# Two mixture-of-experts layers behind linear attention: layer 2's first expert on split weights with the slots stationary, and slot products and copies moved at the end of attention

## The chip, the cores and the metric

The kernel runs on one core of a Trainium2 chip, as one program. The metric is the device time of one execution in microseconds (us). The engines are TensorE (PE in the rows; its weight loads are PEld), VectorE (DVE), ScalarE (ACT), GpSimd (POOL) and SyncE (SP), each with a queue of its own that it works off in order. They wait for each other by semaphores. Loads and stores go through 16 DMA engines, fed by queues on SP, ACT and POOL.

## The reference

Input are q, k, v of 2 batches x 8 heads x 768 positions x 64, and for each of two layers a gate (512 x 8) and the weights w1 (8 x 512 x 1024) and w2 (8 x 1024 x 512) of eight experts, all f32. Linear attention with a decay comes first:

```python
for t in range(S):
    state = gamma[None, :, None, None] * state + np.einsum('bhd,bhe->bhde', k[:, :, t], v[:, :, t])
    y[:, :, t] = scale * np.einsum('bhd,bhde->bhe', q[:, :, t], state)
```

Its output is 1536 tokens of 512 features. Each of the two layers then sends a token to its best expert alone:

```python
expert_idx = np.argmax(x @ w_gate, axis=1)
h = np.maximum(xe @ w1[e], 0.0)        # xe: the tokens of expert e
out[mask] = gate_w[mask, None] * (h @ w2[e])
```

`gate_w` is the softmax probability of the chosen expert. In layer 2 an expert takes its first 384 tokens only and the rest give zero.

## The kernel before, in words

**Tiling.** Tokens go in 12 tiles of 128. Attention ends with the logits of each tile's rows; `step(n, 0..2)` routes tile n: key and one-hot, rank among the tokens of its expert, and the place in the expert's list of slots. The rows of a layer's input lie in memory (`x1d` for layer 1, `x2d` for layer 2), and an indirect DMA of POOL, the gather (L347), fetches the rows of an expert's slots. Each expert has up to 256 slots in the kernel's layout, in tiles of 128 (the second one may be shorter).

**Weights.** An expert has eight slices of 128 x 1024 (512 KB): four of w1 and four of w2. A slice is loaded into `st` by SP, cast by ACT to a short f32 format, `whi` (L159), and DVE subtracts to get the rest, `wlo` (L170). A product then takes three matmuls: x·hi, x·lo and the rest of x times hi. The expert that comes first in a layer is chosen early (`choose`), before all tokens are routed. Its four w1 slices are loaded whole (`load_whole`), without cast and subtraction, and multiplied in full f32 (`products`, L434, weights stationary, 128 or 112 slots moving). Slices are numbered through: 0 to 63 are layer 1's, 64 to 127 layer 2's; slices 64 to 67 are the w1 of layer 2's first expert. SP's load of slice 72 and all behind it waits for the gather of the first expert's second tile.

**The two boundaries.** While the last tokens of a layer's input are routed, PE would have nothing to do. There the products of the first expert's first 128 slots are put between the routing's small matmuls (`ahead_of`, `ahead[1](n)`; each call issues one of eight groups of four f32 matmuls, which the trace shows as eight rows). When the last placement is through (`ig`, L245), `of_first` (L407, L411) picks the row numbers of the second tile, and POOL gathers these rows. `finish_route` (DVE, some 18 small instructions to `over`, L311) sorts the experts and writes the slot lists; the relus (`hidden`: ACT L457, DVE L458) and further products are mixed into it. When the second tile's rows are there, PE turns them (`first_x`, L377), ACT copies them (L378), and the products of the second tile follow. In layer 1, `second()` puts 24 warming matmuls of no use (L374) ahead of that. In layer 2, the output of the first tile (`o_part`, L859 to L861) stands between.

**The last expert.** Layer 2's last expert already does what the change does elsewhere: `hidden_rows` (L820 to L822) keeps the slots stationary and moves 256 columns of the split weights, twelve matmuls per slice; `back_hidden` turns the result back by four transposes (L828), a cast by ACT (L830) and a subtraction by DVE (L831), which give h and its rest. Here the relu comes before (L999).

**What sets the order.** The program is written out in order, so each engine's order is the order of the calls. `between(j, i)` is called after each eighth of an expert and hands out casts and subtractions of the slices to come.

Of the kernel before, what the change touches and what calls it, by code (L numbers as in the profile page):

```python
# [10 lines left out]
F32 = mybir.dt.float32  # L11
F32R = mybir.dt.float32r
# [6 lines left out]
P = 128  # L19
# [60 lines left out]
def fused(ctx, tc, qT, kT, vkr, wg, w11, w12, w21, w22, cst, out, capacity):  # L80
# [44 lines left out]
    def whole(q):  # L125

        return q // 8 % E == 0 and q % 8 < 4
# [343 lines left out]
    with tc.tile_pool(name="ap", bufs=3) as ap:  # L471
# [352 lines left out]
    def back_hidden(hr, h, b):  # L824
# [4 lines left out]
        sl = slice(4 * b, 4 * b + 4)  # L829
        A.copy(h[:, sl, 0, :P], tp)  # L830
        V.tensor_sub(h[:, sl, 1, :P], tp, h[:, sl, 0, :P])  # L831
# [47 lines left out]
    def layer(li, xd, rin):  # L879
# [4 lines left out]
        h = xp.tile([P, KF, 2, C0], F32R, tag="h", name="h", bufs=1)  # L884
# [3 lines left out]
        left = []  # L888
# [7 lines left out]
        def second():  # L896
            x[0] = first_x(rows[0][1], 24)
            go(1)

# [9 lines left out]
        if li == 0:  # L909
            ix = finish_route(rin, li, [None, None, lambda: evac(0), None, None, done])  # L910
            second()
            split()
            evac(1)
            done()
        else:
            ix = finish_route(rin, li, [lambda: evac(0), None, None, done, None, None, lambda: (go(1), evac(1)), None,
                                        done])
            split()
        next_rows(1)
        if li == 1:  # L920
            gate[0][0][0]()
            ps0 = mmtile("o")
            o_part(E * 8, P, h, [ps0], range(0, 6))
            gate[0][0] = gate[0][0][1]()
            x[0] = first_x(rows[0][1])
            o_part(E * 8, P, h, [ps0], range(6, KF))
            put_out(0, 0, P, ps0, gate[0][0][0], ix)

        def between(j, i):
# [29 lines left out]
            if li == 0 and j + 1 == E and i == 4:  # L959
                rt[1]["x"] = first_x(rt[1]["rows"])  # L960
# [6 lines left out]
        def rows_first(j):  # L967

            return li == 1 and j + 1 == E and caps[j] == P

        for j in range(E):
# [6 lines left out]
            for i in range(4):  # L978
                if j == 0:
# [10 lines left out]
                elif rows_first(j):  # L990
                    if i % 2 == 0:
                        ps = mmtile("hr")
                    hidden_rows(q0, x[j], i, ps)
                    run_pend()
                    if i == 2:
                        back_hidden(hr, h, 0)
                    if i % 2:
                        hr = xp.tile([P, 2, C0], F32, tag="hs", name="hr", bufs=2).rearrange("p a c -> p (a c)")
                        A.activation(hr, ps, AF.Relu)  # L999
# [12 lines left out]
            if li == 0:  # L1012
# [7 lines left out]
                for d2 in range(2):  # L1020
# [91 lines left out]
            else:  # L1112
                tiles = halves(cap)[j == 0:]
                ps = [mmtile("o")[:c] for _, c in tiles]
                for i in range(4):
                    o_part(q0, cap, h, ps, (2 * i, 2 * i + 1), int(j == 0))
                    between(j, 4 + i)
# [233 lines left out]
class Halves:  # L1351
# [7 lines left out]
    def half(self, i, bank, xt):  # L1359
# [6 lines left out]

        part = self.rp.tile([P, E], F32, tag=f"lg{i}", name=f"lg{i}")[:self.cnt]
# [7 lines left out]
        o = self.row[:, i * 2 * P:(i + 1) * 2 * P].rearrange("p (j c) -> p j c", j=2)  # L1375
        if gate is None:
            nc.scalar.copy(o, v[:, :, 0:P])
        else:
            nc.scalar.activation(o, v[:, :, 0:P], AF.Copy, scale=gate)
# [46 lines left out]
```

## Time and profile before

| | |
|---|---|
| median of 3 runs | 427.5 us (424.79 to 427.71) |
| profiled execution | 428.34 us, span of its instructions 426.6 us |
| granted TensorE clock, mean | 0.991 |
| PE / weight loads | busy 407.3 us (95%) / 382.0 us |
| DVE | busy 319.1 us (75%) |
| ACT | busy 239.3 us (56%) |
| POOL | busy 96.5 us (23%) |

Times in the rows count from the first instruction of the profiled execution. The boundary from attention to layer 1 lies at about 61 to 74 us, that from layer 1 to layer 2 at 231 to 278 us.

### The profile page before, as it was taken

How to read it: one execution, taken by the hardware profiler on the slowest of the kernel's cores; microseconds unless marked ns; L12 is line 12 of the kernel's file. 1: busy time of each engine (PE TensorE's matmuls, PEld its weight loads, DVE VectorE, ACT ScalarE, POOL GpSimd, SP SyncE). 2: the span in 40 equal slices, each digit the busy share in tenths (PEclk: the TensorE clock that was granted, in tenths of full speed). 3: DMA queues.
4: the chain of work that ended last, by engine and by line, in shares of the span. 5: the costliest groups of instructions: out<-in, count | busy, mean ns of one | idle time of the engine just before them, and what ended most of it. 6: DMA issues, size and time to landing. Idle time of an engine off the chain costs nothing.

```text
span 426.6 us, 9472 instructions
## 1 busy us (share of the span) xinstructions
PE 407.3 (95%) x3403; PEld 382.0 (90%) x3403; DVE 319.1 (75%) x870; ACT 239.3 (56%) x485; POOL 96.5 (23%) x89
## 2 busy tenths in 40 slices
PE   8999989999999999999999999999999999999980
PEld 7887869999999999999999998998889999999970
DVE  3678786788889898989798954677585878787710
ACT  2111221667766666677665622666666787878620
POOL 2334214104041323222100313021304122301120
PEclk9999999999999999999999999999999999999996
DMA  8999974976757576776658615578757777776310
GB/s 316 388 385 390 339 312 136 354 260 223 222 189 246 209 241 226 233 234 231 191 197 265 236 35 190 210 272 284 272 181 253 247 264 241 245 277 233 128 48 16
DMA packets 32503, 100.45 MB, mean 235 GB/s; under 512 B 4669, under 2 KB 5181, under 8 KB 32448
## 3 DMA queue, kind: packets, MB, share of 16 engines
q1 hardware_dynamic: 25488, 82.74, 56.1%
q0 software_dynamic: 4656, 13.00, 8.8%
q10 hardware_dynamic: 2304, 4.02, 2.5%
q8 instruction: 29, 0.48, 0.4%
q14 instruction: 26, 0.21, 0.2%
HBM read 87.01 MB, written 12.99 MB: 234 GB/s over the span
## 4 chain that ended last, share of the span: by engine, by line
PE 80%; DMA 9%; DVE 3%; issue 3%; SPq 1%; ACT 1%; POOL 1%; POOLq 0%; ACTq 0%; DVEq 0%
PE y L844 17%; PE h L800 17%; PE h L801 8%; PE y L845 8%; PE h L434 7%; PE cb L1332 4%; DMA vk<-vkr 3%; PE o L859 3%; PE o L861 3%; PE o L860 3%; PE tp L362 2%; DMA whole<-w 2%; DMA qb<-qT 2%; DMA rows<-x1d,eig 2%; DVE wlo L170 1%
## 5 line engine op out<-in xcount | busy, mean ns | idle before, releaser
L170 DVE TENSOR_TENSOR wlo<-st,whi 128x1024 fp32r<-128x1024 f32 x120 | 145.1, 1217 | 4.1 <-ACT x L378 2.6
L159 ACT CAST whi<-st 128x1024 fp32r<-128x1024 f32 x120 | 125.0, 1045 | 24.9 <-DMA st<-w 24.5
L844 PE MATMUL y<-h,whi 128*128 128x416 f32 (+9 forms) x384 | 116.9, 369 | 0.0
L800 PE MATMUL h<-x,whi 128*128 128x416 f32 (+9 forms) x384 | 114.5, 365 | 0.0
L845 PE MATMUL y<-h,wlo 128*128 128x208 f32 (+9 forms) x384 | 96.9, 252 | 0.0
L801 PE MATMUL h<-x,wlo 128*128 128x208 f32 (+9 forms) x384 | 96.7, 252 | 0.0
L844 PEld LDWEIGHTS y<-h,whi 128*128 128x128 f32 x384 | 72.1, 188 | 2.5 <-DVE rro L232 0.4
L800 PEld LDWEIGHTS h<-x,whi 128*128 128x128 f32 x384 | 72.1, 188 | 2.1 <-issue 0.6
L801 PEld LDWEIGHTS h<-x,wlo 128*128 128x128 f32 x384 | 73.4, 191 | 0.1
L845 PEld LDWEIGHTS y<-h,wlo 128*128 128x128 f32 x384 | 73.4, 191 | 0.0
L321 POOL DMA_INDIRECT x2d<-row,is x16 | 17.4, 1088 | 117.1 <-ACT row L1345 87.7
L812 DVE SCALAR_TENSOR_TENSOR h<-hs,h 128x416 fp32r<-128x416 f32 (+9 forms) x48 | 27.0, 562 | 19.1 <-ACT h L811 15.7
L321 POOL DMA_INDIRECT out<-ob,is x14 | 14.9, 1067 | 111.9 <-ACT ob L865 109.4
L811 ACT ACTIVATE h<-hs 128x416 fp32r<-128x416 f32 (+9 forms) x48 | 25.1, 523 | 25.5 <-DVE hs L786 24.5
L786 DVE TENSOR_TENSOR hs<-h,hb 128x208 f32<-128x208 f32 (+9 forms) x96 | 29.8, 348 | 6.7 <-ACT hb L785 5.0
L434 PE MATMUL h<-x,whole 128*128 128x128 f32 (+1 forms) x256 | 30.8, 278 | 0.7 <-ACT x L378 0.7
L785 ACT COPY hb<-h 128x208 f32<-128x208 f32 (+9 forms) x96 | 27.2, 317 | 6.4 <-PE h L801 5.5
L434 PEld LDWEIGHTS h<-x,whole 128*128 128x128 f32 x256 | 29.4, 192 | 1.3 <-ACT x L378 0.9
L1343 ACT COPY row<-cb 128x512 f32<-128x512 f32 x11 | 6.4, 585 | 40.7 <-DVE lgb L1338 26.7
L347 POOL DMA_INDIRECT rows<-x1d,igs x14 | 23.4, 1673 | 11.0 <-ACT gx L761 5.1
L786 DVE TENSOR_TENSOR yt<-y,yb 128x208 f32<-128x208 f32 (+9 forms) x48 | 15.1, 353 | 14.1 <-ACT yb L785 14.1
L859 PE MATMUL o<-whi,h 128*128 128x512 f32 (+1 forms) x64 | 24.3, 379 | 0.0
(198 smaller groups left out, 612.2 us busy)
## 6 DMA issues: line engine op xcount, KB each, us to landing
st<-w SPq DMA_DIRECT2D x120, 512.0 KB, 4.1
vk<-vkr SPq DMA_DIRECT2D x11, 512.0 KB, 6.0
whole<-w SPq DMA_DIRECT2D x8, 512.0 KB, 6.2
x2d<-zero SPq DMA_DIRECT2D x12, 260.0 KB, 7.2
qb<-qT SPq DMA_DIRECT2D x12, 256.0 KB
x1d<-row ACTq DMA_DIRECT2D x11, 260.0 KB, 5.7
kt<-kT SPq DMA_DIRECT2D x11, 256.0 KB, 5.8
vk<-vkr ACTq DMA_DIRECT2D x1, 512.0 KB
```

The source lines that it names most:

```text
L159: A.copy(hi, st)
L170: V.tensor_sub(lo, st, hi)
L321: ins = nc.gpsimd.indirect_dma_start(dst.rearrange("n (i d) -> (n i) d", i=parts) if parts > 1 else dst[:, :], bass.IndirectOffsetOnAxis(a ...
L434: T.matmul(ps[:, j], w[:, k, j % 2 * P:(j % 2 + 1) * P], x[:, k], start=k == 0, stop=k == KD - 1, skip_group_check=True)
L785: A.copy(b, ps[:, 1, :])
L786: V.tensor_add(out, ps[:, 0, :], b)
L800: T.matmul(ps, hi[:, k, fs], x[:, k, :, :cap], start=k == 0, stop=False, skip_group_check=True)
L801: T.matmul(ps[:, 0, :], lo[:, k, fs], x[:, k, 0, :cap], start=False, stop=k == KD - 1, skip_group_check=True)
L812: V.scalar_tensor_tensor(h[:, sl, 1, :cap], s, 0.0, h[:, sl, 0, :cap], ALU.max, ALU.subtract)
L844: T.matmul(ps[i], hi[:, ds], h[:, f, :, :cap], start=f == 0, stop=False, skip_group_check=True)
L845: T.matmul(ps[i][:, 0, :], lo[:, ds], h[:, f, 0, :cap], start=False, stop=f == KF - 1, skip_group_check=True)
L859: T.matmul(p, h[:, f, 0, ts_], hi, start=f == 0, stop=False)
```

## The change: layer 2's first expert, and the order at both boundaries

Slices 64 to 67 are no longer loaded whole but go through cast and subtraction as all others. The first expert of layer 2 uses `hidden_rows` and `back_hidden` for both of its tiles; its rows are turned by `transposes` (ACT L363, DVE L364, x and its rest) in place of `first_x`. The output of the first tile is cut in three: features' blocks 0 and 1 stand in `finish_route`, 2 and 3 behind it, and 4 to 7 behind the turning of the second tile's rows. Slice 71's cast and subtraction are done in `split()` behind `finish_route`. At the end of attention the place of tile 8 and that of tile 10 move to later points of PE's order, the copies of the last rows (`Halves.half`) are issued before the reduction, and in `second()` one group of products is put ahead of `first_x`, whose warming matmuls go from 24 to 10. In the changed kernel the lines named above stand at L821 to L823 (`hidden_rows`), L827 (relu), L834 (transposes), L836 and L837 (cast, subtraction) and L881 to L883 (`o_part`).

```diff
     def whole(q):
-        return q // 8 % E == 0 and q % 8 < 4
+        return q < 4
...
-        step(NT - 4, 2)
         way = Halves(nc, rp, iw[0], None, P)
 
         def beside(i, xt):
             if i == 0:
+                step(NT - 4, 2)
                 step(NT - 3, 1)
...
         step(NT - 1, 0)
-        step(NT - 2, 2)
         ahead = list(ahead_of(0, rt1))
         ahead[1](1)
+        step(NT - 2, 2)
         step(NT - 1, 1)
...
-    def hidden_rows(q0, x, i, ps):
+    def hidden_rows(q0, x, i, ps, r=0, ks=range(KD)):
...
-        for k in range(KD):
-            T.matmul(o, x[:, k, 0, :P], hi[:, k, :], start=k == 0, stop=False, skip_group_check=True)
-            T.matmul(o, x[:, k, 0, :P], lo[:, k, :], start=False, stop=False, skip_group_check=True)
-            T.matmul(o, x[:, k, 1, :P], hi[:, k, :], start=False, stop=k == KD - 1, skip_group_check=True)
+        sl = slice(r * P, (r + 1) * P)
+        for k in ks:
+            T.matmul(o, x[:, k, 0, sl], hi[:, k, :], start=k == 0, stop=False, skip_group_check=True)
+            T.matmul(o, x[:, k, 0, sl], lo[:, k, :], start=False, stop=False, skip_group_check=True)
+            T.matmul(o, x[:, k, 1, sl], hi[:, k, :], start=False, stop=k == KD - 1, skip_group_check=True)
...
+    def rows_ahead(q0, x):
+        got = []
+        parts = []
+        def go(n):
+            for _ in range(n):
+                if not parts:
+                    b, ps = len(got), mmtile("hr")
+                    got.append(ps)
+                    parts.extend(lambda i=i, ks=ks: hidden_rows(q0, x, i, ps, 0, ks)
+                                 for i in (2 * b, 2 * b + 1) for ks in (range(0, 2), range(2, 4)))
+                parts.pop(0)()
+        return got, go
...
+        def first_o():
+            ps0.append(mmtile("o"))
+            o_part(E * 8, P, h, ps0, range(0, 2))
...
         def second():
-            x[0] = first_x(rows[0][1], 24)
             go(1)
+            x[0] = first_x(rows[0][1], 10)
...
-            ix = finish_route(rin, li, [lambda: evac(0), None, None, done, None, None, lambda: (go(1), evac(1)), None,
-                                        done])
+            ix = finish_route(rin, li, [None, lambda: (go(1), left.append(relu_rows(got[1]))), None, first_o, None,
+                                        lambda: back_hidden(left[0], h, 1)])
             split()
         next_rows(1)
         if li == 1:
             gate[0][0][0]()
-            ps0 = mmtile("o")
-            o_part(E * 8, P, h, [ps0], range(0, 6))
+            o_part(E * 8, P, h, ps0, range(2, 4))
             gate[0][0] = gate[0][0][1]()
-            x[0] = first_x(rows[0][1])
-            o_part(E * 8, P, h, [ps0], range(6, KF))
-            put_out(0, 0, P, ps0, gate[0][0][0], ix)
+            x[0] = rin["x"]
+            transposes(rows[0], x[0], 1)
+            o_part(E * 8, P, h, ps0, range(4, KF))
+            put_out(0, 0, P, ps0[0], gate[0][0][0], ix)
...
-                    if j + 1 == E and d2:
-                        ahead[:] = ahead_of(E * 8, rt[1])
+                        ahead[:] = rows_ahead(E * 8, rt[1]["x"])
...
             run_pend(2)
             ahead[1](3)
+            hr = relu_rows(ahead[0][0])
             run_pend()
             ahead[1](1)
+            rt[1]["h"] = xp.tile([P, KF, 2, C0], F32R, tag="h", name="h", bufs=1)
             run_pend()
-            ahead[1](2)
+            ahead[1](1)
+            back_hidden(hr, rt[1]["h"], 0)
+            ahead[1](1)
```

DVE at the boundary to layer 2, from the last placement on, before (`ig` is the list of slots, `order` the sorted experts):

```order
L245 TENSOR_TENSOR ig_1177<-tbp,tb_1176 128x16
L407 SCALAR_TENSOR_TENSOR oj,of<-ig_1177,one_3339 128x8
L411 CAST ig_4074<-of 128x1
L269 TENSOR_TENSOR key_4082<-cnt,first_3346 128x8
L273 TENSOR_TENSOR t_4084<-key_4082 128x64
```

And in the changed kernel (`th` holds the turned features):

```order
L245 TENSOR_TENSOR ig_1177<-tbp,tb_1176 128x16
L837 TENSOR_TENSOR h<-th,h 128x4x128
L407 SCALAR_TENSOR_TENSOR oj,of<-ig_1177,one_3325 128x8
L411 CAST ig_4095<-of 128x1
L269 TENSOR_TENSOR key_4101<-cnt,first_3332 128x8
L273 TENSOR_TENSOR t_4111<-key_4101 128x64
```

The subtraction of the first turned half, L837, now stands between the placement and the row numbers (L407, L411) for which POOL's gather waits.

PE at the same place in the changed kernel, from the count behind the last placement to the turning of the second tile's rows (L362); `...` stands for further rows of the same kind:

```order
L248 MATMUL cnt<-S_1175,ones_78 128x8
L821 MATMUL hr<-whi,x 128x256
...
L834 MATMUL th<-cs,hr 128x128 x4
L821 MATMUL hr<-whi,x 128x256
...
L881 MATMUL o<-whi,h 128x512
...
L834 MATMUL th<-cs,hr 128x128 x4
L881 MATMUL o<-whi,h 128x512
...
L362 MATMUL tp<-cs,rows 128x128 x4
```

Before, three groups of products (24 rows of the trace), eighteen `o` matmuls and then the turning (L377) stood there. Now six and twelve `hr` matmuls, eight transposes and twelve `o` matmuls stand ahead of the turning.

DVE behind `finish_route`, in the changed kernel:

```order
L311 TENSOR_REDUCE over<-ov 128x1
L170 TENSOR_TENSOR wlo<-st,whi 128x1024
L758 TENSOR_REDUCE gn<-rows 128x1
L767 TENSOR_SCALAR gs<-gs 128x1
L769 RECIPROCAL gt<-gs 128x1
L364 TENSOR_TENSOR x<-tp,x 128x4x128
```

Before, L458 (the second half of h) stood here in place of L170, and no L364. The subtraction of slice 71 and that of the second tile's x are now between `over` and the second tile's matmuls.

## Rows read from the trace of the kernel before

**Rows 1.** The page: busy time by engine, and granted clock in forty slices.
```profile
PE 407.3 (95%) x3403; PEld 382.0 (90%) x3403; DVE 319.1 (75%) x870; ACT 239.3 (56%) x485; POOL 96.5 (23%) x89
...
PEclk9999999999999999999999999999999999999996
```

**Rows 2.** The page: the chain that ended last, by engine; and the costliest group.
```profile
PE 80%; DMA 9%; DVE 3%; issue 3%; SPq 1%; ACT 1%; POOL 1%; POOLq 0%; ACTq 0%; DVEq 0%
...
L170 DVE TENSOR_TENSOR wlo<-st,whi 128x1024 fp32r<-128x1024 f32 x120 | 145.1, 1217 | 4.1 <-ACT x L378 2.6
```

**Rows 3.** Stretches: PE, PEld, DVE, ACT, POOL busy, then clock, DMA share, GB/s.
```profile
70.30:74.00 3.70, 2.97 (x39) 2.78 (x36) 1.83 (x7) 0.78 (x3) 3.06 (x3) 1.00 0.65 229
...
241.00:246.00 5.00, 4.99 (x38) 4.48 (x37) 4.74 (x13) 2.18 (x6) 0.00 (x0) 1.00 0.21 83
```

**Rows 4.** Timeline of PE at layer 2's start: start, duration, work, [idle before].
```profile
255.13 0.34 PE L243 MATMUL tbp<-E,rR 48*128 48x8 f16 x4
...
255.36 2.92 PE L434 MATMUL h<-x,whole 128*128 128x128 f32 x24
...
262.31 0.60 PE L377 MATMUL tp<-cs,rows 128*128 128x128 f32 x4
...
264.14 7.30 PE L434 MATMUL h<-x,whole 128*128 128x128 f32 x64
271.20 0.48 PE L859 MATMUL o<-whi,h 128*128 128x512 f32 x1
```

**Rows 5.** Timeline of PE in layer 2's last expert.
```profile
399.78 0.32 PE L820 MATMUL hr<-whi,x 128*128 128x256 f32 x1
...
401.23 1.07 PE L1088 MATMUL o<-cs,yt 128*128 128x128 f32 x4
...
405.42 0.65 PE L828 MATMUL th<-cs,hr 128*128 128x128 f32 x4
405.82 0.36 PE L820 MATMUL hr<-whi,x 128*128 128x256 f32 x1
```

**Rows 6.** Timeline of ACT there: the cast behind the transposes.
```profile
406.10 0.59 ACT L830 CAST h<-th 128x512 fp32r<-128x512 f32 x1 [0.75 <-PE th L828]
```

**Rows 7.** Timeline of DVE there: the subtraction behind the cast.
```profile
406.72 0.69 DVE L831 TENSOR_TENSOR h<-th,h 128x512 fp32r<-128x512 f32 x1 [2.27 <-ACT h L830]
```

**Rows 8.** Timeline of DVE at layer 2's start.
```profile
255.51 0.17 DVE L245 TENSOR_TENSOR ig<-tbp,tb 128x16 int32<-128x16 f32 x1 [0.43 <-PE cnt L248]
255.72 0.17 DVE L407 SCALAR_TENSOR_TENSOR oj<-ig,one 128x8 f32<-128x8 int32 x1
...
260.27 0.16 DVE L311 TENSOR_REDUCE over<-ov 128x1 f32<-128x8 f32 x1
```

**Rows 9.** Timeline of POOL at layer 2's start.
```profile
256.86 1.06 POOL L347 DMA_INDIRECT rows<-x2d,ig  x1 [3.00 <-DVE at L275]
```

**Rows 10.** DMA engines' busy tenths from 256 to 262 us, forty slices.
```profile
DMA  0000000000000000099268962000000000009463
```

**Rows 11.** Timeline of PE: the program's start, and attention's end.
```profile
1.07 4.45 PE L464 MATMUL warm<-ones 128*128 128x128 f16 x40 [1.07 <-DVE ones L461]
...
65.53 4.71 PE L434 MATMUL h<-x,whole 128*128 128x128 f32 x40
70.08 1.50 PE L374 MATMUL tp<-ones 128*128 128x128 f16 x24
71.42 0.55 PE L377 MATMUL tp<-cs,rows 112*128 112x112 f32 x4
71.81 1.07 PE L434 MATMUL h<-x,whole 128*128 128x128 f32 x8
73.62 0.81 PE L434 MATMUL h<-x,whole 128*128 128x112 f32 x5 [0.73 <-ACT x L378]
```

**Rows 12.** Timeline of ACT: the copies of the turned rows, at both boundaries.
```profile
73.22 0.59 ACT L378 COPY x<-tp 128x224 f32<-128x224 f32 x2 [4.97 <-PE h L434]
...
262.73 0.65 ACT L378 COPY x<-tp 128x256 f32<-128x256 f32 x2 [1.21 <-PE tp L377]
```

More of the change, by code (lines that the diff above doesn't have):

```diff
@@ L813, in hidden_group, with relu_rows, back_hidden @@
         beside()
-    def hidden_rows(q0, x, i, ps):
+    def hidden_rows(q0, x, i, ps, r=0, ks=range(KD)):
         hi, lo = (t.rearrange("p (k f) -> p k f", k=KD) for t in wq[q0 + i])
         o = ps[:, i % 2 * 2 * P:(i % 2 + 1) * 2 * P]
-        for k in range(KD):
-            T.matmul(o, x[:, k, 0, :P], hi[:, k, :], start=k == 0, stop=False, skip_group_check=True)
-            T.matmul(o, x[:, k, 0, :P], lo[:, k, :], start=False, stop=False, skip_group_check=True)
-            T.matmul(o, x[:, k, 1, :P], hi[:, k, :], start=False, stop=k == KD - 1, skip_group_check=True)
-    def back_hidden(hr, h, b):
+        sl = slice(r * P, (r + 1) * P)
[3 more added lines that the diff above has]
+            T.matmul(o, x[:, k, 1, sl], hi[:, k, :], start=False, stop=k == KD - 1, skip_group_check=True)
+    def relu_rows(ps):
+        hr = xp.tile([P, 2, C0], F32, tag="hs", name="hr", bufs=2).rearrange("p a c -> p (a c)")
+        A.activation(hr, ps, AF.Relu)
+        return hr
+    def back_hidden(hr, h, b, r=0):
         tp = mmtile("th").rearrange("p (f c) -> p f c", f=4)
@@ L828, in back_hidden @@
             T.transpose(tp[:, f, :], hr[:, f * P:(f + 1) * P], ident)
-        sl = slice(4 * b, 4 * b + 4)
-        A.copy(h[:, sl, 0, :P], tp)
-        V.tensor_sub(h[:, sl, 1, :P], tp, h[:, sl, 0, :P])
+        sl, cl = slice(4 * b, 4 * b + 4), slice(r * P, (r + 1) * P)
+        A.copy(h[:, sl, 0, cl], tp)
+        V.tensor_sub(h[:, sl, 1, cl], tp, h[:, sl, 0, cl])
+    def rows_ahead(q0, x):
[10 more added lines that the diff above has]
+        return got, go
     def w2of(q0, f):
@@ L883, in layer @@
         held[(li * E + 1) * 8] = gathers[-1]
-        h = xp.tile([P, KF, 2, C0], F32R, tag="h", name="h", bufs=1)
+        h = rin.get("h") or xp.tile([P, KF, 2, C0], F32R, tag="h", name="h", bufs=1)
         gate = {0: [gates(r) for r in ([rows[0][0]], [rows[0][1]])]}
@@ L887, in layer @@
         got, go = ahead
-        left = []
+        left, ps0 = [], []
+        def first_o():
+            ps0.append(mmtile("o"))
+            o_part(E * 8, P, h, ps0, range(0, 2))
         def evac(b):
@@ L959, in between @@
             if li == 0 and j + 1 == E and i == 4:
-                rt[1]["x"] = first_x(rt[1]["rows"])
+                rt[1]["x"] = new_x()
+                transposes([rt[1]["rows"]], rt[1]["x"], 0)
             if j + 1 < E and i == 6:
@@ L967, in rows_first @@
         def rows_first(j):
-            return li == 1 and j + 1 == E and caps[j] == P
+            return li == 1 and (j == 0 and caps[j] == C0 or j + 1 == E and caps[j] == P)
         for j in range(E):
@@ L978, in layer @@
             for i in range(4):
-                if j == 0:
+                if j == 0 and li == 0:
                     if i % 2 == 0:
@@ L992, in layer @@
                         ps = mmtile("hr")
-                    hidden_rows(q0, x[j], i, ps)
+                    r = int(j == 0)
+                    hidden_rows(q0, x[j], i, ps, r)
                     run_pend()
                     if i == 2:
-                        back_hidden(hr, h, 0)
+                        back_hidden(hr, h, 0, r)
                     if i % 2:
-                        hr = xp.tile([P, 2, C0], F32, tag="hs", name="hr", bufs=2).rearrange("p a c -> p (a c)")
-                        A.activation(hr, ps, AF.Relu)
+                        hr = relu_rows(ps)
                     between(j, i)
@@ L1116, in layer @@
                     o_part(q0, cap, h, ps, (2 * i, 2 * i + 1), int(j == 0))
+                    if j == 0 and i == 0:
+                        back_hidden(hr, h, 1, 1)
                     between(j, 4 + i)
@@ L1365, in half @@
         v = bank.rearrange("p (j c) -> p j c", j=2)
+        o = self.row[:, i * 2 * P:(i + 1) * 2 * P].rearrange("p (j c) -> p j c", j=2)
+        if gate is None:
+            nc.scalar.copy(o, v[:, :, 0:P])
         part = self.rp.tile([P, E], F32, tag=f"lg{i}", name=f"lg{i}")[:self.cnt]
@@ L1374, in half @@
                 nc.vector.tensor_scalar(self.lg, self.lg, gate, None, ALU.mult)
[L1375 to L1378, printed above, removed]
+        if gate is not None:
             nc.scalar.activation(o, v[:, :, 0:P], AF.Copy, scale=gate)
```

## The prediction

> **What bounds the kernel now.** The page comes first. PE is busy 95% of the span and its granted clock stands at the full level in every slice until the end [rows 1]; the chain that ended last is PE for 80% [rows 2]. So time is won by issuing less on PE, or by closing the few places where it waits, and work added to the other engines costs only where PE comes to wait for it. The change touches two such places, so I read next the timelines of all engines there: attention's end and the start of layer 2.
>
> At attention's end PE has first-tile products from 65.53, the warming matmuls from 70.08, the turning of the second tile's rows at 71.42, eight more product rows, and then it stands 0.73 us until ACT's copies let it go on at 73.62 [rows 11]. The copies start at 73.22, which is 1.80 after the turning began, while at the other boundary the same pair started 0.42 after it (262.73 against 262.31) [rows 4, 12]. Nothing else is on ACT there: it was idle for 4.97 us [rows 12].
>
> At layer 2's start PE never waits behind the last placement. Placement at 255.13, 24 product rows, 18 output matmuls, the turning at 262.31, the rest of the output, 64 product rows from 264.14, and the second tile's output at 271.20 [rows 4]. The gather that this needs is released by DVE's L407 at 255.72 [rows 8], starts on POOL at 256.86 [rows 9], and its last full stretch of DMA ends in the 25th of 40 slices of 0.15 us, near 259.75 [rows 10], 2.5 us before the turning. That is the slack of the present order.
>
> **The change, part by part.**
>
> *PE's work in layer 2's first expert.* A tile of 128 slots took 64 product rows in 271.20 - 264.14 = 7.06 us, 0.110 each [rows 4]. The last expert shows the new form: twelve matmuls of one slice from 399.78 to 401.23, 1.45 us, and four transposes 405.42 to 405.82, 0.40 us [rows 5]. A tile is then 4 x 1.45 + 2 x 0.40 = 6.6 us, 0.46 less, about 0.9 for both. That is the whole direct gain there, and it counts only where PE does not wait instead.
>
> *The gather of the second tile comes later.* DVE's L837 is put between the placement and L407. L837 needs the cast of the turned features, which needs transposes that stand behind six more matmuls on PE. I keep the placement at 255.13 and the small products behind it to 255.36 [rows 4]. Six matmuls are half of 1.45, so the transposes start at 256.08. The cast starts 406.10 - 405.42 = 0.68 later [rows 5, 6], the subtraction 406.72 - 406.10 = 0.62 behind that [rows 6, 7], so at 257.38, and it lasts 0.69, of which the next one sees about 0.6: L407 at 258.0, against 255.72, which is 2.3 us later. POOL's gather followed L407 by 256.86 - 255.72 = 1.14 and its rows came 2.9 after that [rows 8 to 10]: 259.1 and 262.0.
>
> *PE meanwhile.* From 255.36: 0.72 (six matmuls), 0.40 (transposes), 1.45 (twelve), six outputs, 0.40, six outputs. An output matmul is (262.31 - 255.36 - 24 x 0.110) / 18 = 0.24 [rows 4], six are 1.43. The sum is 5.8, so PE is at the second tile's rows at 261.2 and waits for them 0.8 us. From 262.0: turning 0.40 (as the four transposes above), twelve outputs 2.86, so 265.3.
>
> *DVE's tail.* L407 to `over` took 260.27 - 255.72 = 4.55 [rows 8], with one L458 of 0.7 in it, whose place one L837 of the same length now takes. From 258.0 this ends at 262.6. Then come slice 71's subtraction, 1.22 us [rows 2], needed by the last six output matmuls at about 263.8, so just in time, and, behind two small gate steps, the subtraction of the second tile's x, done at about 265.6. The matmuls that need it stand at 265.3: a wait of 0.3. The second tile's matmuls, 5.8, and one set of transposes, 0.4, end at 271.75, against 271.20; the other set stands inside the output, 0.4 more. This boundary: 0.55 + 0.4, **+0.9 us**.
>
> *Casts and subtractions.* Four more of each. ACT is at 56% and takes them without trouble. DVE is full before the boundary: 4.74 of 5 us from 241 to 246, with PE at 4.99 [rows 3]. One more subtraction there can hold PE by 0 to 1.2 us. I take 0, because what follows is the routing chain, in which the placement waited for DVE (0.43 the other way at `ig` [rows 8]), and later matmuls fill up what is left; 1.2 stays as an end of the range. SP's loads keep their bytes. The loads held by the gather start 2.3 us later; the first slice behind it is used by the second expert, behind the second tile's 24 output matmuls, 24 x 0.24 = 5.8 us, which covers it. Without that cover the second expert would wait for its weights by up to 2.3 us.
>
> *Attention's end.* The eight product rows move ahead of the turning: 48 rows at (70.08 - 65.53) / 40 = 0.114 end at 71.0. Ten warming matmuls at (71.42 - 70.08) / 24 = 0.056 end at 71.56 [rows 11]. If the copies follow the turning by 0.42, as at 262.73 [rows 4, 12], they start at 71.98, and the products 0.40 behind that (73.62 - 73.22 [rows 11, 12]), at 72.4 in place of 73.62: **-1.2 us**. The nearest row for no gain is the same copies at 73.22: whatever held them for 1.4 us may hold them again, which makes 0. I take the gain, because the work ahead of the copies was the only thing that the row names as their releaser (PE's products, L434), and this work is now ahead of the turning. The moved placements and the copy ahead of its reduction change the order on PE and ACT only; the chain through DVE from tile to tile stays. 0, with 0.3 either way.
>
> **Sum.** -1.2 + 0.9 = -0.3 us on the profiled execution's 428.34, so 428.0. The median of the runs shown lies 0.84 below that execution: **427.2 us**.
>
> One rule speaks against the fewer warming matmuls. The granted clock was 1.00, the 2.4 GHz level, from 70.3 to 74.0, with PE busy 2.97 of 3.70 us [rows 3]. The program's first 40 warming matmuls took 4.45 us, twice the spacing of the later 24 [rows 11], so the slow level showed in the matmuls there and cost 2.2 us. In the changed order PE stands between turning and products no longer than now, 0.4 us against 0.73, so I put its return at nothing in the sum. The Trainium skill, "TensorE: Matmul & The Clock Gate", Part 1 on the clock gate, says that the throttled clock is the default and that only activity keeps it released. By that rule, fewer useless matmuls ahead of a wait may drop the clock; the trace agrees that a start from idle is slow and shows no drop at this place.
>
> **The rivals.**
>
> *The gather stays hidden.* If the transposes, cast and subtraction go through faster, or rows land earlier, PE runs without a wait: from 255.36 the new work sums to 5.8 + 0.4 + 2.86 + 6.2 + 0.4 = 15.7, against 15.84 before; and the 30 matmuls ahead of the placement (3.6 us) replace 40 rows (4.4), which gives up to 0.8 more if the placement moves up. So -0.1 to -0.9, and with the -1.2 about -1.8: 425.7. For it speaks the slack of 2.5 us in the present order; against it, that L837's place uses 2.3 of it while PE arrives 1.1 earlier.
>
> *Slower: DVE decides layer 2's start.* The one more subtraction ahead of the boundary goes in full, 1.22, into the chain from placement to L407. Everything behind shifts, the rows land at 263.2, and the boundary costs 2.1. It decides from the point where rows land after 262.3, since there the cost passes the 1.2 won at attention's end. Price: +0.9, so 428.4. For it speaks DVE's 4.74 of 5; against it, that DVE has gaps soon after, where PE's products hold up the ranks.
>
> *The copies stay late.* No gain at attention's end, +0.9 in all: 428.4.
>
> *The clock falls once.* Half of 4.45 us is lost: 427.2 + 2.2 = 429.4.
>
> **How the numbers follow.** Chances: forecast 0.45, hidden gather 0.25, DVE 0.13, late copies 0.13, clock 0.04. The likeliest case has 427.2 with about 1 us either way from the terms left at 0. The range for 8 in 10 reaches from the hidden gather with its full 0.8 (427.5 - 1.2 - 0.9 = 425.4, less one us for the runs' own spread, in which one of three lay at 424.79) to the late cases with 0.7 more: 424.3 to 429.1. A change of under 1%, 4.3 us, is about what a measurement of this kernel can't tell from none. No case alone reaches it; two or three together would: faster 0.09, within 1% 0.87, slower 0.04.
>
> **What would show it.** In the changed profile: L407 near 258 and the gather near 259.1; PE idle before L362 for 0.5 to 1 us with the DMA named as releaser; a short wait before the second tile's first `hr` matmul; the second tile's output 15.5 to 17 us after the placement. At attention's end, copies some 0.4 us behind the turning and products at 72.4. The prediction is wrong if PE does not wait before L362, if the copies come more than a us after the turning, or if the experts behind the boundary, which I leave unchanged, differ in length.

## The result, and the profile after

The changed kernel took 429.7 us (median of 12 runs, 428.46 to 432.13), the kernel before 427.61 beside it (12 runs, 424.79 to 431.58): a ratio of 1.0058, 95% interval 1.0041 to 1.0074. By the medians it is 2.1 us slower, where 427.2 was forecast, and it lies outside the range of 424.3 to 429.1. The profiled execution took 430.95 us with a span of 428.6, against 428.34 and 426.6 before. Three of the executions below, one each in experiments 3 and 4 (there the profiled one) and one of the kernel before, took 731.66, 1329.4 and 2195.05 us and are left out of medians and ratios.

**Layer 2's start.** The timeline of PE in the changed kernel (start, duration, work, idle time and its releaser), against [rows 4]:

```profile
255.15 0.34 PE L243 MATMUL tbp<-E,rR 48*128 48x8 f16 x4 [0.24 <-DVE rR L234]
...
256.17 0.60 PE L834 MATMUL th<-cs,hr 128*128 128x128 f32 x4
...
259.42 0.60 PE L834 MATMUL th<-cs,hr 128*128 128x128 f32 x4
...
262.66 0.63 PE L362 MATMUL tp<-cs,rows 128*128 128x128 f32 x4 [1.26 <-DMA rows<-x2d,ig]
...
272.36 0.39 PE L881 MATMUL o<-whi,h 128*128 128x512 f32 x1
```

DVE there, against [rows 8], and POOL, against [rows 9]:

```profile
255.53 0.18 DVE L245 TENSOR_TENSOR ig<-tbp,tb 128x16 int32<-128x16 f32 x1 [0.43 <-PE tbp L243]
257.42 0.69 DVE L837 TENSOR_TENSOR h<-th,h 128x512 fp32r<-128x512 f32 x1 [1.72 <-ACT h L836]
258.03 0.15 DVE L407 SCALAR_TENSOR_TENSOR oj<-ig,one 128x8 f32<-128x8 int32 x1
...
263.32 0.16 DVE L311 TENSOR_REDUCE over<-ov 128x1 f32<-128x8 f32 x1
263.40 1.22 DVE L170 TENSOR_TENSOR wlo<-st,whi 128x1024 fp32r<-128x1024 f32 x1
```
```profile
259.16 1.06 POOL L347 DMA_INDIRECT rows<-x2d,ig  x1 [4.69 <-DVE at L275]
```

This is the chain that was foreseen: the subtraction at 257.42 stands between placement and L407, the gather starts at 259.16, and PE now waits 1.26 us for its rows, where 0.8 was forecast.

**Attention's end.** PE and ACT in the changed kernel, against [rows 11, 12]:

```profile
66.72 5.60 PE L434 MATMUL h<-x,whole 128*128 128x128 f32 x48
72.17 0.72 PE L374 MATMUL tp<-ones 128*128 128x128 f16 x10
72.72 0.55 PE L377 MATMUL tp<-cs,rows 112*128 112x112 f32 x4
73.52 1.15 PE L434 MATMUL h<-x,whole 128*128 128x112 f32 x8 [0.24 <-ACT x L378]
```
```profile
73.12 0.59 ACT L378 COPY x<-tp 128x224 f32<-128x224 f32 x2 [3.68 <-PE tp L377]
```

The copies (73.12) do come 0.40 us behind the turning (72.72), as forecast. But everything ahead of them is about 1.2 us later than in the profile before (48 products from 66.72, 40 from 65.53 before). Part of that is a new wait. DVE's reduction of the last tile's logits, in the changed kernel and then in the kernel before:

```profile
63.52 0.17 DVE L1404 TENSOR_REDUCE lg<-ca 128x8 f32<-128x16 f32 x1 [1.21 <-ACT row L1402]
```
```profile
62.34 0.17 DVE L1368 TENSOR_REDUCE lg<-ca 128x8 f32<-128x16 f32 x1 [0.59 <-PE rk L223]
```

The copy that the change writes ahead of the reduction reads the same bank, and the reduction now waits for it; the copy itself stands behind two others on ACT (the turned rows of another tile).

**The end.** ACT and PE among the last experts of the changed kernel:

```profile
388.82 1.05 ACT L159 CAST whi<-st 128x1024 fp32r<-128x1024 f32 x1 [1.60 <-DMA st<-w]
...
405.64 1.05 ACT L159 CAST whi<-st 128x1024 fp32r<-128x1024 f32 x1 [2.10 <-DMA st<-w]
```
```profile
397.03 0.41 PE L866 MATMUL y<-h,whi 128*128 128x320 f32 x1 [0.39 <-DVE h L812]
...
408.36 0.66 PE L834 MATMUL th<-cs,hr 128*128 128x128 f32 x4 [0.75 <-ACT hr L827]
```

Weights come late for these two of ACT's last casts; the relu is queued behind the cast at 405.64, and PE waits for it. SP issued its last load at 400.29, at 397.46 before. Two neighbouring loads of SP, in the changed kernel and then in the kernel before:

```profile
389.00 0.33 SPq L138 DMA_DIRECT2D st<-w  x1
392.97 0.33 SPq L138 DMA_DIRECT2D st<-w  x1
```
```profile
387.50 0.33 SPq L138 DMA_DIRECT2D st<-w  x1
390.13 0.33 SPq L138 DMA_DIRECT2D st<-w  x1
```

Counted from the second expert's first matmul (279.25 and 277.75), the first of the two is issued at the same time in both, 109.75; the second is 1.34 us later in the changed kernel.

**Where the time lies.** From such rows each profiled execution is cut into stretches, by PE: up to the ninth tile's logits, to the last placement count (L248), to layer 1's first `y`, to its third expert, to its eighth expert's `y`, to layer 2's second expert, to the last matmul, to the end of the span, and the time outside the span (us).

```
                       logits  count   y1   3rd   y(8)  2nd,L2  last  tail   out
before, as shown        47.97  17.54 15.27 34.61 121.76  40.60 135.77 13.08 1.74
before, second profile  48.55  17.95 14.27 35.01 121.72  40.60 135.69 11.91 1.75
before, third profile   48.12  17.69 14.28 34.56 121.70  40.62 135.68 12.95 1.73
the change              48.34  18.36 13.99 35.20 121.74  41.62 137.23 12.12 2.35
layer-2 part alone      47.91  18.03 14.27 34.58 121.75  41.63 136.68 13.15 2.37
layer 2, gather first   47.95  17.60 14.27 34.99 121.75  39.91 135.71 13.12 1.86
change, gather first    48.20  17.85 14.83 34.63 121.77  39.88 136.20 13.24 2.42
```

### The profile page after: what moved, and what is told of

The parts are those of the page before. It is cut to its first block, busy times and chain, and to the rows that moved or that the text cites. A ratio compares the mean times of both kernels' runs of the same rounds, so it can differ in the third digit from the quotient of the medians.

```text
span 428.6 us, 9427 instructions
## 1 busy us (share of the span) xinstructions
PE 405.9 (95%) x3373; PEld 379.4 (89%) x3373; DVE 324.6 (76%) x876; ACT 244.1 (57%) x491; POOL 96.9 (23%) x89
## 4 chain that ended last, share of the span: by engine, by line
PE 69%; DVE 10%; DMA 10%; issue 3%; ACT 3%; SPq 1%; POOL 1%; POOLq 0%; ACTq 0%; DVEq 0%
PE y L866 16%; PE h L800 14%; PE y L867 7%; PE h L801 6%; PE cb L1365 4%; PE h L434 3%; DVE wlo L170 3%; DMA kt<-kT 3%; DMA st<-w 3%; PE tp L362 3%; PE o L881 2%; PE o L883 2%; PE o L882 2%; DMA whole<-w 2%; DMA rows<-x1d,eig 2%
## 5 line engine op out<-in xcount | busy, mean ns | idle before, releaser
L170 DVE TENSOR_TENSOR wlo<-st,whi 128x1024 fp32r<-128x1024 f32 x124 | 149.9, 1216 | 3.9 <-ACT whi L159 3.9
L159 ACT CAST whi<-st 128x1024 fp32r<-128x1024 f32 x124 | 129.3, 1046 | 27.5 <-DMA st<-w 26.9
L347 POOL DMA_INDIRECT rows<-x1d,igs x14 | 24.4, 1743 | 8.8 <-issue 4.7
L881 PE MATMUL o<-whi,h 128*128 128x512 f32 (+1 forms) x64 | 24.2, 378 | 0.0
L883 PE MATMUL o<-whi,h 128*128 128x512 f32 (+1 forms) x64 | 23.5, 367 | 0.0
L882 PE MATMUL o<-wlo,h 128*128 128x512 f32 (+1 forms) x64 | 23.5, 366 | 0.0
```

What stands on the lines that cost most here:

```text
L159: A.copy(hi, st)
L170: V.tensor_sub(lo, st, hi)
L881: T.matmul(p, h[:, f, 0, ts_], hi, start=f == 0, stop=False)
L882: T.matmul(p, h[:, f, 0, ts_], lo, start=False, stop=False)
L883: T.matmul(p, h[:, f, 1, ts_], hi, start=False, stop=f == KF - 1)
```

## The experiments

Line numbers of rows are those of the kernel that ran. Each time stands beside the kernel before on the same chip (427.2 to 428.3 from batch to batch), and the ratio is to that.

**1. Copy behind the reduction again** (the changed kernel otherwise).

```
-        o = self.row[:, ...]; if gate is None: nc.scalar.copy(o, v[:, :, 0:P])   # ahead of tensor_reduce
+        ... the same, behind tensor_reduce, as before
```


> The changed kernel, with one edit undone: the copies of the last rows stand behind the reduction again (ScalarE's copy was issued ahead of VectorE's reduction of the same bank). Theory: the reduction of the first half's logits waited 1.21 us for ScalarE's copy, itself queued behind the copies of the turned rows; undone, that wait falls to about 0.6 (as before), the last placement comes 0.4 us earlier and with it the gather, the held weights and the first experts: 429.0 to 429.3, 0.4 to 0.7 us under the changed kernel. Rival: the late placement at attention's end is only a late start of the execution, and the wait moves to another place: same time as the changed kernel, 429.7.

429.47 us (9 runs), ratio 1.0038 [1.0020, 1.0056]. From the first matmul of the bank's second logits to the last count it is 3.27 us, as in the kernel before, against 3.68 in the change. The wait of 0.41 is gone, but the interval overlaps that of the change, so the time doesn't decide.

**2. Gather first**: L837's subtractions go behind the instructions that lead to the gather.

```
-        V.tensor_sub(h[:, sl, 1, cl], tp, h[:, sl, 0, cl])
+        sub = lambda: V.tensor_sub(h[:, sl, 1, cl], tp, h[:, sl, 0, cl])   # called in finish_route behind sel
```


> The changed kernel, with the subtractions of the first tile's turned features moved on VectorE alone: the first from ahead of the row numbers to behind the sorting's fourth step, the second to behind finish_route. TensorE's and ScalarE's order and the amount of work stay. Theory: the gather then starts near 256.9 in place of 259.2, TensorE does not wait for its rows (1.26 us before), slice 71 is split 0.8 us earlier, the held weight loads start 2.3 us earlier, and the waits of the last two experts (0.4 and 0.75 us and the late subtractions) go: 426.5 to 427.5, that is 2 to 3 us under the changed kernel. Rival: the four more subtractions and the new form of the matmuls cost the time, wherever they stand: 429 to 430 with an early gather. Second rival: only the 1.3 us of TensorE's wait comes back and the end stays late: 428.4.

429.01 us (12 runs), 1.0037 [1.0019, 1.0055]. The boundary falls to 39.88, 1.74 less than in the change and 0.72 less than before; the time as a whole does not follow as far. It lies in the range of the rival that the new form costs its time wherever the subtractions stand; experiment 5 speaks against that rival.

**3 and 4. Attention's edits alone, and of them only the second half** (`go(1)` ahead of `first_x`, warming 24 to 10).

> The kernel before with all edits at attention's end (two placements moved, copies ahead of the reduction, one group of products ahead of the turning, 10 warming matmuls) and nothing of layer 2. Theory: what the earlier copies win (1.2) is spent by the later placement (0.4 to 0.6) and by the held weights coming as much later: 427.0 to 427.8, no change. Rival: this part carries the loss of 2 us: 429 to 430. Rival: the earlier copies win in full: 426.4.

> The kernel before with one edit: in layer 1 the group of eight product rows ahead of the turning of the second tile's rows, and 10 warming matmuls in place of 24. Theory: ScalarE's copies follow the turning by 0.4 us in place of 1.8 and the second tile's products start 1.2 us earlier; the placement, the gather and the held weights stay where they were, so what follows is 1.2 earlier as long as weights are there: 426.4 to 426.8. Rival: the second expert waits for its weights, which come no earlier, and the gain is gone by then: 427.6. Rival: the fewer warming matmuls let the clock fall: 429 or more, with a granted clock below 1.00 between 70 and 80 us.

428.66 us, 1.0022 [0.9998, 1.0047], and 428.86 us, 1.0021 [1.0003, 1.0039]. What should have given 1.2 us gives nothing; whether it costs anything these two intervals hardly tell. **The second half again, with profiles, beside the unchanged kernel:**

> The kernel before, unchanged, for a second profile and as a measure of the noise. All theories: 427.2 to 428.2, ratio 1.000 within 0.002. On the time from the turning of the second tile's rows to that tile's first product (2.20 us in the first profile): theory A (the first profile was an unlucky one; as a rule the eight product rows behind the turning hide the copies): 1.4 to 1.5 us. Theory B (the copies are late in most executions): 1.8 to 2.2 us.

> The same kernel as e4 (one edit: the group of products ahead of the turning, 10 warming matmuls), whose profile was disturbed. Theory A (as a rule the copies were hidden before, and now the whole time from turning to product, 0.8 us or more, lies open): 428.5 to 429, with 0.8 to 2 us from turning to product and the placement where it was. Theory B (e4's 1.2 us was noise): 427.2 to 428. Theory C (fewer warming matmuls let the clock fall): a granted clock of 0.5 in a stretch between 70 and 80 us in the profile.

> The kernel before once more, for a third profile: theory A: 1.4 to 1.5 us from turning to product in two profiles of three; theory B: 1.8 or more in all.

> The kernel of e6 once more, for another profile: theory A: second tile's first product 7.4 us or more behind the last placement, as late as or later than in the kernel before; theory B: 6.9 to 7.3, earlier than before.

The unchanged kernel against itself: 427.33 us, 0.9999 [0.9980, 1.0019]. The second half again: 428.21 us, 1.0026 [1.0001, 1.0052]. The two single executions: 427.33 and 431.29, the latter with a granted clock of 0.5 for 3.4 us from 64.3, after 2.3 us in which PE was busy for 1.04. The two new profiles of the kernel before settle the main question: there the copies follow the turning by 0.4 us, and from count to `y1` it is 14.27 and 14.28, not the 15.27 of the profile that I predicted from. Against them the second half gains 0.29 us.

**5. Layer 2's part alone, and with the gather first.**

> The kernel before with the layer-2 part of the change alone (the first expert on split weights, slots stationary, features turned back sooner), attention as before. Theory of separate prices: the boundary of the layers costs 1.05 us as in the changed kernel, the end of the last experts 0.3, the time outside the span 0.5, so 429.0 to 429.3 against 427.3 for the kernel before. Rival, attention's edits carry half of the loss: 428.3 or less.

> The kernel before with the layer-2 part alone, the two subtractions of weight remainders moved behind the instructions that lead to the gather, attention as before. Theory: the boundary is 0.7 us shorter than before, the weights' waits at the end take 0.4 back, the time outside the span costs 0.5: 427.3 to 427.8, no difference to the kernel before. Rival, the boundary's gain reaches the end: 426.6. Rival, a queue held up by the late loads: over 428.3.

428.79 us, 1.0041 [1.0023, 1.0059], and 427.31 us, 1.0009 [0.9987, 1.0031]; 12 runs each. So layer 2's part loses about 1.6 us by itself, and the order of two subtractions is most of it: between the two kernels lie 1.48 us by the medians and 1.72 (41.63 against 39.91) at the boundary in their profiles. POOL, DVE and PE with the gather first:

```profile
255.83 1.06 POOL L347 DMA_INDIRECT rows<-x2d,ig  x1 [2.41 <-PE th L834]
```
```profile
254.69 0.17 DVE L407 SCALAR_TENSOR_TENSOR oj<-ig,one 128x8 f32<-128x8 int32 x1
...
256.39 0.69 DVE L837 TENSOR_TENSOR h<-th,h 128x512 fp32r<-128x512 f32 x1 [0.48 <-ACT h L836]
```
```profile
260.22 0.60 PE L362 MATMUL tp<-cs,rows 128*128 128x128 f32 x4
```

The gather is 1.7 us behind the placement at 254.11 in place of 4.0, and PE turns the second tile's rows without a wait.

**6. Does the longer time outside the span depend on the streams' length?** The same with 16 tiny memsets on DVE and 16 tiny copies on ACT at the start.

> The same kernel with 16 tiny memsets on DVE and 16 tiny copies on ACT added at the program's start, which shift the place of every later instruction in the instruction streams and do nothing else. Theory that a fetch of instructions falls behind the last instruction only for some lengths of a stream: no fetch after the end, time outside the span 1.8 instead of 2.25, so 0.5 us less than the run without the additions. Rival, the longer time outside belongs to the layer-2 part whatever the length: 2.2 to 2.4 as before, no gain.

434.77 us. The padding was ill placed: ACT's copies stand ahead of its first loads, which are issued at 5.39 instead of 0.75, and the start is 7 us longer. Outside the span the profiled execution took 1.87, but its sister without padding has 1.86 too. By the runs, none of 5 has more than 2 us there against 4 of 12 without padding, which so few runs don't tell apart; nothing is decided by it.

**7. The short warming alone** (24 to 10 in the kernel before).

> The kernel before with 10 instead of 24 small warming matmuls at attention's end, so that the turning behind them comes up to 0.8 us sooner; nothing else changed. Theory that the second expert's weights bind behind it: from the last placement count to layer 1's first y up to 0.8 us less, from there to the third expert's h as much more, 427.3 to 427.8, no change. Rival, the time reaches the end: 426.6. Rival, the clock falls for lack of the warming: over 428.5.

427.94 us, 1.0014 [0.9995, 1.0033]. In its profile 13.50 from count to `y1`, 0.78 less, and 34.80 behind it. The weights gave back little there in that execution, against my theory; yet the runs show no gain, and why is open.

**8. Attention's other edits one by one**: the copy ahead of the reduction; the products ahead with 24 warming matmuls; the moved placements.

> The kernel before with one of attention's edits alone: ACT's copy of the last slice's two halves is written ahead of DVE's reduction of the same bank. Theory that the reduction then waits for the copy: DVE's second reduction at the bank waits for ACT instead of PE, the last placement count comes 0.4 us later, 427.5 to 427.8 against 427.2 for the kernel before. Rival, something later waits longer anyway and hides it: 427.2.

> The kernel before with the eight products of the second half moved ahead of the turning, the 24 warming matmuls kept. Theory that these products were the cover of the copies behind the turning: the next product waits 0.2 to 0.3 us for a prompt copy and about 1 us for a late one, so 427.4 to 428.2. Rival, the loss of the products and the short warming together came from the warming: 427.2.

> The kernel before with the placement steps of the second and fourth last slices moved as in the change, nothing else. Theory that they lie beside other work either way: 427.2, no difference, last placement count within 0.2 us of the kernel before. Rival, a step now stands ahead of the bank's reduction on DVE: last count up to 0.7 us later and 427.9.

1.0008 [0.9988, 1.0029], 1.0016 [0.9996, 1.0036], 1.0007 [0.9981, 1.0033]. None can be told from no change by itself; their excesses sum to 0.0031, against 0.0022 for all together. With the copy ahead, the reduction waited for ACT and the last count came 0.43 us later behind the bank's logits, as expected. In all three profiles the copies of the turned rows came late (0.99 to 1.83 us behind the turning; 0.4 is called prompt here). POOL, PE and ACT with the moved placements (late), then in the third profile of the kernel before (prompt):

```profile
70.80 1.03 POOL L347 DMA_INDIRECT rows<-x1d,igs  x1 [2.22 <-issue]
72.14 1.68 POOL L347 DMA_INDIRECT rows<-x1d,igs  x1 [0.30 <-issue]
74.13 1.02 POOL L347 DMA_INDIRECT rows<-x1d,igs  x1 [0.30 <-issue]
```
```profile
71.90 0.55 PE L377 MATMUL tp<-cs,rows 112*128 112x112 f32 x4
73.73 0.59 ACT L378 COPY x<-tp 128x224 f32<-128x224 f32 x2 [5.00 <-PE h L434]
```
```profile
70.63 1.03 POOL L347 DMA_INDIRECT rows<-x1d,igs  x1 [2.22 <-issue]
71.97 1.68 POOL L347 DMA_INDIRECT rows<-x1d,igs  x1 [0.30 <-issue]
73.95 1.87 POOL L347 DMA_INDIRECT rows<-x1d,igs  x1 [0.30 <-issue]
```
```profile
71.73 0.55 PE L377 MATMUL tp<-cs,rows 112*128 112x112 f32 x4
72.12 0.59 ACT L378 COPY x<-tp 128x224 f32<-128x224 f32 x2 [3.57 <-PE tp L377]
```

In the late case the copy begins at 73.73, just before POOL's second gather ends at 72.14 + 1.68 = 73.82. So it is in all five profiles in which both copies are late: 0.04 to 0.16 before that end. In two more (experiments 1 and 2) the first copy began 0.93 and 0.95 us behind the turning and the second apart from it, 0.14 and 0.13 before that gather's end. The prompt copies begin 0.15 to 0.27 after the gather's start, so the two meet in either case, and the outcome differs from execution to execution. Late are 7 of the 15 profiles in which they meet; with the short warming alone the copies are prompt and begin 0.63 us ahead of the gather.

**9. The gather held until the copies are through**: in the kernel before, in layer 2's part with the gather first, and with the products moved ahead.

```
             if r and behind is not None:
+                nc.gpsimd.tensor_copy(cp.tile([P, 1], F32, name="seen"), behind)   # behind: x[0][:, KD-1, 0:1]
             out.append(take(xd, ig[...], cnt))
```


> The kernel before, where POOL's gather of the second expert's rest waits, behind a small POOL copy of one column of the turned features, until ACT's two copies are through. Theory that this gather holds the copies up: they begin 0.4 us behind the turning in every execution, from the last placement count to layer 1's first y 14.3 us; the median falls by the share of late executions times 1 us, so 426.5 to 427.0 where the kernel before has 427.2 to 428.0 (up to 0.9 us less). Rival, the copies come late for another reason: late ones are seen again, no change of the median. Rival, the gather's rows then come too late for the second expert: 0.5 us or more slower.

> The layer-2 part with the gather first, and in attention the same held gather. Theory as before: copies prompt, and 0.3 to 0.9 us less than the kernel before. Rival: no difference to the kernel before.

> The products of the second half ahead of the turning with 24 warming matmuls, and the gather held. Theory: TensorE waits 0.2 to 0.3 us for the copies and never 0.8, so from the last placement count to layer 1's first y 14.6 to 14.8 us instead of 15.35, and the time that of the kernel before within 0.5 us. Rival: 15.3 again and 0.5 to 0.8 us slower than the kernel before.

426.99 us (8 runs), **0.9963 [0.9948, 0.9978]**; 426.79 us (6 runs), **0.9958 [0.9942, 0.9973]**; 428.45 us (12 runs), 0.9998 [0.9980, 1.0016]. POOL, ACT and PE of the first:

```profile
72.20 1.04 POOL L347 DMA_INDIRECT rows<-x1d,igs  x1 [2.22 <-issue]
74.36 0.18 POOL L358 COPY seen<-x 128x1 f32<-128x1 f32 x1 [1.12 <-ACT x L383]
75.22 1.28 POOL L347 DMA_INDIRECT rows<-x1d,igs  x1 [0.68 <-issue]
```
```profile
73.69 0.59 ACT L383 COPY x<-tp 128x224 f32<-128x224 f32 x2 [3.57 <-PE tp L382]
```
```profile
73.30 0.55 PE L382 MATMUL tp<-cs,rows 112*128 112x112 f32 x4
73.69 2.51 PE L439 MATMUL h<-x,whole 128*128 128x128 f32 x21
```

Copies 0.4 us behind the turning in all three; from count to `y1` 14.28, 14.28 and 14.77, where 14.3 and 14.6 to 14.8 were expected. By their ratios the first two beat both the kernel before and the change. Their gain, 1.3 to 1.5 us by the medians, is larger than the share of late executions times 1 us explains (at most 0.9 was expected), and no profile shows where it is won: the profiled execution of the first was the slowest of its eight, 428.51 us. With 7 of 15 late, three prompt profiles would come by chance about one time in seven (an estimate, (8/15) to the third), and the held gather itself comes 1.7 us later behind the turning. So the experiment speaks for the gather as the cause of late copies and doesn't prove it; that holding it saves time is shown for the first two kernels, and in the third there is no gain over the kernel before.

## Why the prediction was wrong, by its steps

*Attention's end, -1.2 us: this step failed.* I compared with one execution in which the copies were late by chance, and took the order of the work ahead of them as the cause because the row names PE's products as releaser. Two more profiles of the kernel before have the copies at 0.4 us, hidden behind the eight products. Against those the edit gains 0.29 us up to `y1`, and in the three profiles that have this gain the stretch behind it, to the third expert, is 35.20 to 35.94 us against 34.56 to 35.01, so it doesn't last. Besides, the products that moved ahead were part of the cover: copies 1.4 us later cost 1.0 in the kernel before (15.27 against 14.27), copies 1.25 later cost 1.25 with attention's edits (15.24 against 13.99). My rival "the copies stay late" had the right doubt and the wrong picture: they are late in some executions of either order.

*The copy ahead of the reduction, at 0 with 0.3 either way: wrong in kind.* I said that the chain through DVE stays. It gained a wait for ACT, worth 0.41 to 0.52 us on the way to the last count in all four profiles with the copy ahead.

*Layer 2's start, +0.9: the sum was right, and partly by luck.* The order of events came as forecast: L407 at 258.03 (forecast 258.0), the gather at 259.16 (259.1; its row names L275 on DVE as releaser and not L407, but from L407 to the gather it is 1.13 to 1.14 us before, in the change and with the gather first), a wait of 0.2 us for the rest of x (0.3). Two things came later: `over` at 263.32 (262.6), because the second L837 waits for its cast, and the rows, turned at 262.66 (262.0). From the placement to the second expert it became 24.10 us in place of 22.62, 1.48 more where 0.9 was forecast. But the placement, which I kept where it was, came 0.46 sooner behind layer 1's eighth expert (17.52 us in place of 17.98), which only the rival of the hidden gather had as possible. Together the stretch to the second expert grew by 1.02 us.

*The held loads, covered by 5.8 us of output matmuls: right, but the last experts are not unchanged.* The second expert did not wait. SP's first load behind the gather came at 262.73, at 260.42 before, which is 0.8 us later counted from the second expert. But the loads caught up: counted so, the 41st load from the last and the fifth from the last are issued at the same time in both kernels to within 0.02 us. What stretches the end comes later. In the changed kernel the seventh and eighth loads from the last took 7.1 and 6.9 us from issue to landing, in the third profile of the kernel before 4.9 and 4.3, and from the fourth on SP's loads are 1.3 us late. A later last load is seen in kernels whose layer 2 is unchanged, too (us; "behind it" counts from the second expert to that load, the last column from the second expert to the last matmul; the last three rows are experiments 7, 4 and 8, with layer 2 as before):

```
                        second expert  last load issued   behind it   to last matmul
before                      277.75          397.46          119.71        135.77
layer-2 part alone          278.17          398.82          120.65        136.68
the change                  279.25          400.29          121.04        137.23
layer 2, gather first       276.47          396.38          119.91        135.71
short warming alone         276.49          396.80          120.31        135.81
second half, third          280.57          401.01          120.44        135.70
copy ahead alone            278.03          398.71          120.68        136.76
```

A late last load goes with a longer end in some of them, and not in all. So the 1.5 us that the changed kernel's profile has more there can't be put down to the late gather, and one profile of each kernel doesn't tell how much of it is that execution's chance. Why single loads land late is open.

*Outside the span: not in the prediction.* It took 1.73 to 1.92 us in 130 runs of the kernel before in five batches, but about 2.3 in 7 of the 12 of the change, and 2.1 to 2.4 in some or all runs of each kernel with the layer-2 part but the padded one. In the profiles with 2.3 one packet of instructions is fetched about 2 us after the last instruction:

```profile
q14 instruction: 1, 0.01, 0.5%
```

It costs 0.3 us on the mean of the 12 runs. That the layer-2 part causes it is suggested by the kernels in which it occurs, not shown.

*The clock: right.* The mean granted clock was 0.9893 in the change and 0.9895 in 130 runs of the kernel before, and from 70 to 80 us it was 1.00 in all seven undisturbed profiles with 10 warming matmuls. The Trainium skill's rule that I weighed ("TensorE: Matmul & The Clock Gate", Part 1) would have had fewer warming matmuls lower it; no run shows that. The slow level that I read from the spacing of the first 40 warming matmuls is not in the rows of the clock: from 1.0 to 5.5 us the granted clock reads 1.00 there, so that price of 2.2 us is not shown by them.

**Together**, by the profiles with prompt copies: 0.4 to 0.8 to the last count, -0.3 from there to `y1`, 0.2 to 0.6 to the third expert, 1.0 at the boundary, up to 1.5 from there to the last matmul, 0.3 outside. The sum is 3 to 4 us, with up to 1 us of a shorter tail against it; the tail alone differs by 1.2 us between executions of the kernel before, so the sum stands to the measured 2.1 only within about 1 us. By the runs, layer 2's part costs 1.6 us by itself, where 0.9 was forecast: 1.0 of it is the boundary and 0.2 the time outside the span, and the rest has no place. Attention's edits, which should have won 1.2, cost about 0.9 (with an interval that just reaches none). Why they cost anything is open.

**What stays open** is why the copies escape POOL's gather in some executions, and what they contend for. The Trainium skill, "Trainium Architecture — The Big Picture", section "What this means for kernel authors", says that among the engines only DVE and GpSimd contend for a port to SBUF. By that ScalarE's copies should run beside the gather. The runs don't show a port: they show three of three profiles prompt with the gather out of the way, where 7 of 15 were late.

## What to carry to other kernels

A wait in one profile may be one execution's luck: before a gain is built on it, look at it in a second profile of the same kernel. Work that stands behind a short dependent step may be what hides it; moving it ahead turns an irregular delay into a wait of the bound engine. When a step would stand between a count and a gather, put the gather first. And where a late load at the end is to be put down to an early delay, count the loads from a common event and see whether the delay lasts on the way; here it didn't.

## What the runs showed of the hardware that was not expected

ACT's copies from PSUM were late beside POOL's indirect gather in 7 of 15 profiles: up to 1.4 us later, in five of them beginning as the 1.68 us gather ends, in the other two with the second copy there. Two engines that only read one PSUM bank ran one after the other in this program: the reduction waited 1.21 us for the copy. Whether the chip or the program's semaphores order them was not separated. And the time outside the span has two values, 1.8 and 2.3 us, the longer with an instruction fetch behind the last instruction.
